# A windowed-attention and two-MLP kernel: another written order of the first part's tasks, and other engines for some of them

## Chip, cores and metric

One NeuronCore of a Trainium2 chip runs the kernel; the other cores are idle. The metric is the device time of one execution in microseconds (us), lower is better. Engines are named as in the profile: PE (TensorE matmul), PEld (its weight load), DVE (VectorE), ACT (ScalarE), POOL (GpSimd) and SP (SyncE, which here only issues DMA transfers). A name with q (SPq) is an engine's sequencer.

## What is computed

```python
# attention, B=4 H=8 S=576 D=64: a windowed one plus one on 4x down-sampled q, k, v
q_d, k_d, v_d = (t.reshape(B, H, S//4, 4, D).mean(axis=3) for t in (q, k, v))
out_up = np.repeat(softmax_attn(q_d, k_d, v_d), 4, axis=2)
mask = np.abs(pos[:, None] - pos[None, :]) < 4
out_local = softmax_attn(q, k, v, where=mask)
x = tokens_by_heads(out_up + out_local)      # (2304, 512)
h = x @ w_in                                 # 512 x 2048
y = (h * np.cos(h)) @ w_out                  # 2048 x 512
out = ((y @ w_a) * (y @ w_b)) @ w_out2       # 512 x 1536, 1536 x 512
```

All of it is in float32. The kernel makes a float32 product from three matmuls over a high and a low part of each operand.

## The kernel before, in words

**Two parts.** The first part holds the attention, the first MLP, and the preparation of the second MLP's weights. The second part, the second MLP, is a chain of matmuls whose operands are formed by ACT, POOL and DVE beside it; the change doesn't touch its instructions. In the first part everything is a *task* with a name, and a long string, `ORDER` (from line 48), lists 2663 task names. The loop at line 957 goes through the string and calls each task, and `InOrder.settle` (line 212) chains the instructions of each engine, SP among them, so that they run on the engine in just that written order. A suffix `@a`, `@d` or `@p` puts an operation on ACT, DVE or POOL where the kernel can do it on any of them.

**Attention tasks.** A unit u (0 to 7) is half a sequence of one batch entry; each has pairs of heads (last figure of a name). `lp` makes the local scores (PE, L402), `lm` masks them and takes the maximum (DVE, L409, L414), `lu` subtracts it (L419), `le`, `ln`, `lz` are the exponential, the sum and the division, `lt` transposes (PE, L497), `lc` copies the transposed scores out of PSUM (L299 on DVE, L297 on ACT). The same on down-sampled data is `sm` (sums of four, one instruction L379 on DVE or three, L381 to L383, on POOL), `dp` (PE, L426), `dx` (maximum, DVE, L432), `da`, `de`, `dn`, `dz`, `dt` (PE, L509), `dc`. `vp` sums v (PE, L350; `vs`, L370 on DVE, L372 and L374 on POOL, does this for later units). `at` multiplies by v (PE, L522, L529), `up` and `cb` (L545) combine both results in SBUF, `xh` and `xl` split them into high and low. One PSUM buffer named "att" holds scores, transposes or results of one step at a time.

**MLP tasks.** A group g (0 to 111) is 128 columns of the hidden layer for one block of tokens. `h{g}.0` to `.3` are its products (`h_mm`, three matmuls each, L595 to L597), in one of two PSUM buffers "h". Stages `c{g}.0` to `.5` make h·cos h: ACT L646, DVE L648, ACT L650, DVE L652 (which releases the PSUM buffer), then the high part (L297 or L299) and the low part (L658). `b{g}.0` to `.3` multiply by w_out into four accumulators, `e` and `S` copy out and store them.

**Weights.** They arrive as 64-bit words and are rebuilt: `w{n}.0` to `.4` for the first MLP (L273, L276 on ACT, L278 on DVE, then high and low). For the second MLP a block n (0 to 32) goes through `p{n}.0` (load, SP, L805), `.10`, `.11`, `.12` (rebuild, ACT L273 and L276, DVE L278), `.2` (four sums on POOL, L814 to L817) and `.5` (store, SP, L838). Below n = 24 the odd blocks share one buffer "praw" (a single one), and the even ones take whatever buffer of the pool "w" comes free, so a load waits on SP until an earlier block is stored.

Of the kernel before, what the change touches and what calls it, by code (L numbers as in the profile page):

```python
# [48 lines left out]
L0k0 L0k1 lp0.0 sm0.0@d L0w1 w1.1@a w1.0@a L0v0 sm0.1@d lm0.0 lu0.0@p dp0.0 dx0.0 L0k3 lu0.1@d da0.00@d da0.01@d le0.0 ln0.0 de0.0 dn0.0 dz0.1@a  # L49
dz0.0@d lz0.0@d L0V0 vp0.0 vq0.0@a vq0.1@a L0k2 sm0.2@d dt0.0 w1.2@d dc0.0@a L0w2 w2.0@a w2.1@a lt0.0 lc0.01@a lc0.00@d L0w0 w0.1@a L0w4 sm0.3@p  # L50
w1.3@d w1.4@p w2.2@d dp0.1 dx0.1 da0.10@d w0.0@a at0.0 up0.0@d cb0.1 cb0.0 w2.3@a w4.0@a w0.2@d w0.3@d da0.11@a w4.1@a w4.2@d w2.4@p L0v1 lp0.1 lm0.1
lu0.3@d lu0.2@d xh0.1@a w0.4@p L0w5 L0w6 w5.1@a w5.0@a w5.2@d xl0.1@d xh0.0@a xl0.0@p w6.0@a L0V1 vp0.1 w6.1@a Lc8 h0.0 Lc9 h0.1 de0.1 dn0.1 dz0.3@p
le0.1 ln0.1 vq0.3@a w6.2@d lz0.1@d Lk2.0 vq0.2@a Lq1.0 sm1.0@p Lq1.1 sm1.1@p dz0.2@a h1.0 h1.1 dt0.1 dc0.1@d w9.0@a w4.3@a lt0.1 lc0.10@d w9.1@a
w9.2@d w8.0@a w6.3@d w6.4@p lc0.11@a at0.1 up0.1@d cb0.2 L0w3 cb0.3 xh0.3@d w5.3@a w3.0@a w3.1@a xh0.2@a w8.1@a L0w7 w7.0@a xl0.2@d h0.2 Lc10 xl0.3@d
w7.1@a Lq1.3 Lk2.1 Lc11 Lw2.0 Lk2.2 Lc14 h0.3 w3.2@d w3.3@a w9.3@d w3.4@p w5.4@p w7.2@d c0.0@a c0.1@d lp1.0 lm1.0 lu1.1@d lu1.0@p w10.1@a h1.2 h1.3
dp1.0 c0.2@a c0.3@d w4.4@p c1.0@a c1.1@d w7.3@a c1.2@a dx1.0 Lq1.2 c0.4@a c1.3@d da1.00@d h2.0 da1.01@d h2.1 w7.4@d c0.5@p c1.4@d c1.5@p le1.0 w8.2@d
# [36 lines left out]
c33.0@a c33.1@d c33.2@a c33.3@d xh3.2@d c30.5@p lp4.0 lm4.0 lu4.0@d h32.2 h32.3 c32.0@a c32.1@d c32.2@a h34.0 h34.1 h34.2 Lp30 b28.0 b30.1 Lq4.2
c33.4@d lu4.1@p c33.5@d Lw4.3 b29.3 c32.3@d h34.3 c34.0@a c34.1@d vs4.3@p xl3.2@p dp4.0 dx4.0 da4.00@d da4.01@a b30.2 b29.0 Lw4.4 vs4.4@p b30.0 h35.0
# [1152 lines left out]
```

## Time and profile before

| | us |
|---|---|
| median of 3 runs (905.39 to 907.26) | 906.39 |
| the profiled execution | 908.52 |
| its span, first to last instruction | 906.8 |
| PE busy | 884.1 (97%) |
| DVE, ACT, POOL busy | 675.3, 559.3, 507.2 |
| mean granted clock of TensorE | 0.992 |

The span lies inside the execution's own time, with 1.7 us around it. PE is the busiest engine. A stall is written in a trace as the idle time in brackets ahead of an instruction, with the work that ended it. The first part ends near 515 us.

### The profile page before, as it was taken

The page shows a single profiled execution, that of the slowest core. Times are in us where ns is not written, and L with a number is a line of the kernel's source. Part 1 is how long each engine was busy: PE and PEld are TensorE (multiplying, and loading weights), DVE is VectorE, ACT ScalarE, POOL GpSimd, SP SyncE. Part 2 cuts the span into 40 slices and gives each one's busy share as a digit, 9 for nine tenths or more (in the row PEclk, how much of TensorE's full clock was granted, in tenths as well). Part 3 has the DMA queues.
Part 4 walks back from the last instruction along what each step waited for, and adds up shares of the span by engine and source line. Part 5 has one row for each costly group of instructions (what it writes and reads, how often), then busy time and mean ns, then how long its engine had stood idle before and what let it go on. Part 6 is the DMA issues. An engine that isn't in the chain of part 4 may idle for free.

```text
span 906.8 us, 19124 instructions
## 1 busy us (share of the span) xinstructions
PE 884.1 (97%) x7020; PEld 858.1 (95%) x7020; DVE 675.3 (74%) x1295; ACT 559.3 (62%) x1172; POOL 507.2 (56%) x662
## 2 busy tenths in 40 slices
PE   5899999999999999999999999999999999999998
PEld 5789899999998998999999999999999999999998
DVE  7999898775876877734766688778867787776764
ACT  6999876575586765634665355466654477545473
POOL 5687755653566556302464267654586663677540
PEclk9799999999999999999999999999999999999999
DMA  9793322543756656102978166676742456832631
GB/s 352 278 353 109 103 64 64 183 147 91 222 175 203 216 182 192 46 1 64 289 220 274 63 203 209 209 314 241 290 153 85 154 205 250 323 113 89 228 143 53
DMA packets 96909, 162.13 MB, mean 179 GB/s; under 512 B 6576, under 2 KB 62896, under 8 KB 96816
## 3 DMA queue, kind: packets, MB, share of 16 engines
q1 hardware_dynamic: 96816, 160.92, 52.0%
q8 instruction: 55, 0.90, 0.4%
q14 instruction: 38, 0.31, 0.1%
HBM read 127.66 MB, written 33.23 MB: 177 GB/s over the span
## 4 chain that ended last, share of the span: by engine, by line
PE 78%; DMA 8%; DVE 4%; ACT 4%; POOL 3%; issue 2%; SPq 0%; ACTq 0%; POOLq 0%; DVEq 0%
PE z L595 14%; PE z L597 14%; PE z L596 14%; PE h L595 5%; PE acc L595 5%; PE h L596 5%; PE h L597 5%; PE acc L597 5%; PE acc L596 5%; DMA praw<-in_w_b_dram 2%; DMA wd_a<-praw 2%; DMA vs<-in_vds_dram 1%; PE att L402 1%; DVE praw L278 1%; DMA praw<-in_w_out_dram 1%
## 5 line engine op out<-in xcount | busy, mean ns | idle before, releaser
L991 POOL TENSOR_TENSOR sb<-w,sb 128x256 fp32r<-128x256 f32 x154 | 124.7, 822 | 115.2 <-ACT sb L989 112.0
L595 PE MATMUL h<-xbig,w 128*128 128x288 f32 (+1 forms) x448 | 145.2, 324 | 5.3 <-DVE gs L652 3.5
L595 PE MATMUL acc<-gh,w 128*128 128x288 f32 (+1 forms) x448 | 144.2, 322 | 0.0
L596 PE MATMUL h<-xbig,w 128*128 128x288 f32 (+1 forms) x448 | 141.5, 316 | 0.0
L597 PE MATMUL h<-xbig,w 128*128 128x288 f32 (+1 forms) x448 | 141.0, 315 | 0.0
L596 PE MATMUL acc<-gl,w 128*128 128x288 f32 (+1 forms) x448 | 140.3, 313 | 0.3 <-POOL gl L658 0.2
L597 PE MATMUL acc<-gh,w 128*128 128x288 f32 (+1 forms) x448 | 140.1, 313 | 0.2 <-POOL w L588 0.2
L989 ACT ACTIVATE sb<-w 128x256 fp32r<-128x256 f32 x252 | 96.6, 415 | 50.1 <-PE z L597 39.8
L658 POOL TENSOR_TENSOR gl<-gs,gh 128x288 fp32r<-128x288 f32 (+1 forms) x62 | 59.1, 956 | 92.7 <-ACT gh L297 49.3
L596 PE MATMUL z<-xbig,sb 128*128 128x384 f32 x288 | 96.2, 334 | 0.0
L595 PE MATMUL z<-xbig,sb 128*128 128x384 f32 x288 | 96.2, 334 | 0.0
L597 PE MATMUL z<-xbig,sb 128*128 128x384 f32 x288 | 96.2, 334 | 0.0
L595 PEld LDWEIGHTS h<-xbig,w 128*128 128x128 f32 x448 | 84.8, 189 | 10.8 <-DVE gs L652 6.0
L595 PEld LDWEIGHTS acc<-gh,w 128*128 128x128 f32 x448 | 84.2, 188 | 3.8 <-issue 1.3
L650 ACT ACTIVATE gs<-gs,turn 128x288 f32<-128x288 f32 (+1 forms) x112 | 63.4, 568 | 38.3 <-DVE gs L648 37.5
L596 PEld LDWEIGHTS h<-xbig,w 128*128 128x128 f32 x448 | 85.1, 190 | 1.2 <-DVE xbig L569 0.2
L596 PEld LDWEIGHTS acc<-gl,w 128*128 128x128 f32 x448 | 84.3, 188 | 1.9 <-POOL gl L658 0.7
L597 PEld LDWEIGHTS h<-xbig,w 128*128 128x128 f32 x448 | 84.9, 190 | 1.0
L597 PEld LDWEIGHTS acc<-gh,w 128*128 128x128 f32 x448 | 84.2, 188 | 1.5 <-POOL w L588 0.4
L646 ACT ACTIVATE gs<-h,turn 128x288 int32<-128x288 f32 (+1 forms) x112 | 58.9, 528 | 41.9 <-PE h L597 38.8
L648 DVE SCALAR_TENSOR_TENSOR gs<-gs,h 128x288 f32<-128x288 int32 (+1 forms) x112 | 54.9, 492 | 38.7 <-ACT gs L646 38.3
L991 DVE TENSOR_TENSOR sb<-w,sb 128x256 fp32r<-128x256 f32 x98 | 62.1, 635 | 22.0 <-ACT sb L989 22.0
(177 smaller groups left out, 2381.5 us busy)
## 6 DMA issues: line engine op xcount, KB each, us to landing
w<-wd SPq DMA_DIRECT2D x63, 512.0 KB, 5.9
w<-wd_a SPq DMA_DIRECT2D x18, 512.0 KB, 6.9
w<-wd_b SPq DMA_DIRECT2D x18, 512.0 KB, 7.6
raw<-in_w_in_dram SPq DMA_DIRECT2D x16, 512.0 KB, 7.2
raw<-in_w_out_dram SPq DMA_DIRECT2D x16, 512.0 KB, 7.9
w<-wd_a SPq DMA_DIRECT2D x18, 384.0 KB, 7.7
w<-wd_b SPq DMA_DIRECT2D x18, 384.0 KB, 6.7
praw<-in_w_a_dram SPq DMA_DIRECT2D x12, 512.0 KB, 3.4
```

The costliest lines, as they stand in the source:

```text
L278: dve.scalar_tensor_tensor(out=lw if out is None else out, in0=hh, scalar=3, in1=lw, op0=ALU.logical_shift_left, op1=ALU.bitwise_or)
L402: pe.matmul(p[i][o, W * w:W * w + W], qt[u, 2 * pr + i][r, off:off + W], kt[u // 2, 2 * pr + i][r, BASE[half] + off:BASE[half] + off + W], ...
L595: i = pe.matmul(ps_out, lh, rh, start=start, stop=False, skip_group_check=more)
L596: pe.matmul(ps_out, lh, rl, start=False, stop=False, skip_group_check=more)
L597: pe.matmul(ps_out, ll, rh, start=False, stop=stop, skip_group_check=more)
L646: act.activation(out=gs[g].bitcast(I32), in_=hps[g], func=AF.Identity, scale=1.0 / (2.0 * math.pi), bias=turn[:, 0:1])
L648: dve.scalar_tensor_tensor(out=gs[g], in0=gs[g].bitcast(I32), scalar=-2.0 * math.pi, in1=hps[g], op0=ALU.mult, op1=ALU.add)
L650: act.activation(out=gs[g], in_=gs[g], func=AF.Sin, bias=turn[:, 1:2])
L658: eng.tensor_tensor(out=gl[g], in0=gs.pop(g), in1=gh[g].bitcast(F32), op=ALU.subtract)
L989: act.activation(out=t[:, 0], in_=blk, func=AF.Copy)
L991: (dve if nst[0] % (C["SD"] if G else C["SD0"]) == 0 else pool).tensor_tensor(out=t[:, 1], in0=blk, in1=t[:, 0].bitcast(F32), op=ALU.subtract)
```

## The change

Only the string `ORDER` differs: the same 2663 tasks in another order, with other engine marks. Two places of it, the start, and the lines around p9 to p11:

```diff
-L0k0 L0k1 lp0.0 sm0.0@d L0w1 w1.1@a w1.0@a L0v0 sm0.1@d lm0.0 lu0.0@p dp0.0 dx0.0 L0k3 lu0.1@d da0.00@d da0.01@d le0.0 ln0.0 de0.0 dn0.0 dz0.1@a
...
+L0k0 L0k1 lp0.0 sm0.1@d L0w1 w1.1@a w1.0@a lm0.0 L0v0 L0k3 sm0.0@p dp0.0 dx0.0 da0.01@a da0.00@d L0V0 vp0.0 lu0.1@p sm0.3@d lu0.0@p L0w2 le0.0 ln0.0
...
-Lw6.2 vs6.2@p lt5.1 lc5.11@a h61.2 h61.3 lc5.10@a c61.0@a b59.3 c61.1@d c61.2@a c61.3@d b59.0 dt5.1 dc5.1@a h63.0 h63.1 h63.2 c62.4@d h63.3 c63.0@a
-c61.4@a c61.5@d c62.5@p c63.1@d p11.0 p11.11 p11.10 p11.12 p11.2 h64.0 b59.1 h64.1 h64.2 b59.2 b60.2 c63.2@a c63.3@d h64.3 c64.0@a at5.1 up5.1@a b60.0
...
+xl5.1@d p10.0 p10.11 p10.10 p10.12 c62.4@a c62.5@d h63.0 p9.5 xl5.0@p h63.1 h63.2 c61.1@d h63.3 c63.0@a c63.1@d dt5.1 dc5.1@a b58.3 b59.3 b60.3 b58.1
+c61.2@a c61.3@d c61.4@d c61.5@d b59.0 p10.2 b59.1 c63.2@a at5.1 up5.1@a cb5.2 Lw6.2 vs6.2@p c63.3@d xh5.2@d xl5.2@d b59.2 cb5.3 p11.0 p11.10 p11.11
```

Operations by engine, before and after (a: ACT, d: DVE, p: POOL):

| task | before | after |
|---|---|---|
| `lu` | d 14, p 18 | d 5, p 27 |
| `sm` | d 18, p 14 | d 21, p 11 |
| `vs` | d 7, p 11 | d 4, p 14 |
| `e` (copies out) | a 24, d 16 | a 17, d 23 |
| `lc` | a 17, d 15 | a 20, d 12 |
| `xl` | d 10, p 22 | d 14, p 18 |
| `up` | a 6, d 10 | a 10, d 6 |

The number of matmuls is the same, and so is that of ACT's table loads (24).

**Start of POOL.** The first places on POOL after the constants (`smx` are local scores, `kd` and `qd` the sums of four, `w` a weight). Before:

```order
L675 MEMSET smd 72x12x16
L419 TENSOR_TENSOR smx<-smx,mx 128x5x64
L381 TENSOR_TENSOR kd<-kq 128x144
L382 TENSOR_TENSOR kd<-kd,kq 128x144
L383 TENSOR_TENSOR kd<-kd,kq 128x144
L381 TENSOR_TENSOR qd<-kq 128x72
L382 TENSOR_TENSOR qd<-qd,kq 128x72
L383 TENSOR_TENSOR qd<-qd,kq 128x72
L588 TENSOR_TENSOR w<-raw,w 128x512 x3
```

Now:

```order
L675 MEMSET smd 72x12x16
L381 TENSOR_TENSOR kd<-kq 128x144
L382 TENSOR_TENSOR kd<-kd,kq 128x144
L383 TENSOR_TENSOR kd<-kd,kq 128x144
L381 TENSOR_TENSOR qd<-kq 128x72
L382 TENSOR_TENSOR qd<-qd,kq 128x72
L383 TENSOR_TENSOR qd<-qd,kq 128x72
L419 TENSOR_TENSOR smx<-smx,mx 128x5x64 x2
L490 TENSOR_TENSOR smd<-smd,sd 72x6x48
L588 TENSOR_TENSOR w<-raw,w 128x512 x3
```

POOL's sums now belong to the first pair of heads (`sm0.0`, before `sm0.3`) and come first, and two subtractions `lu` follow instead of one.

**DVE behind the result of unit 1's first pair of heads** (`at1.0`; `xf<-att` are `up` and `cb`, `gs` the cosine, `sd` sums for a softmax, `w<-raw` a weight). Before:

```order
L299 COPY xf<-att 128x144
L648 SCALAR_TENSOR_TENSOR gs<-gs,h 128x288
L545 TENSOR_TENSOR xf<-att,xf 128x288
L480 TENSOR_SCALAR sd<-sd 72x4
L481 RECIPROCAL sd<-sd 72x4
L299 CAST w<-raw 128x512
L545 TENSOR_TENSOR xf<-att,xf 128x288
L652 TENSOR_TENSOR gs<-gs,h 128x288
```

Now:

```order
L648 SCALAR_TENSOR_TENSOR gs<-gs,h 128x288 x2
L299 COPY xf<-att 128x144
L545 TENSOR_TENSOR xf<-att,xf 128x288 x2
L480 TENSOR_SCALAR sd<-sd 72x4
L481 RECIPROCAL sd<-sd 72x4
L299 CAST w<-raw 128x512
L652 TENSOR_TENSOR gs<-gs,h 128x288
```

The two combining operations, behind which the PSUM buffer "att" is free, follow the copy at once, and the three others come after them.

**ACT from the rebuilding of p11 to that of p12** (the two `praw` rows at either end; `gs<-h` is the first stage of one MLP group). Before:

```order
L276 ACTIVATE praw<-praw,turn 128x512
L273 ACTIVATE praw<-praw 128x512
L650 ACTIVATE gs<-gs,turn 128x288
L646 ACTIVATE gs<-h,turn 128x288
L297 ACTIVATE xf<-att 128x144
L650 ACTIVATE gs<-gs,turn 128x288
L297 ACTIVATE xbig<-xf 128x288 x2
L273 ACTIVATE praw<-praw 128x512
L276 ACTIVATE praw<-praw,turn 128x512
```

Now:

```order
L273 ACTIVATE praw<-praw 128x512
L276 ACTIVATE praw<-praw,turn 128x512
L646 ACTIVATE gs<-h,turn 128x288
L650 ACTIVATE gs<-gs,turn 128x288
L297 ACTIVATE gh<-gs 128x288
L646 ACTIVATE gs<-h,turn 128x288
L650 ACTIVATE gs<-gs,turn 128x288
L297 ACTIVATE xbig<-xf 128x288
L646 ACTIVATE gs<-h,turn 128x288
L276 ACTIVATE praw<-praw,turn 128x512
L273 ACTIVATE praw<-praw 128x512
```

Three MLP groups begin between the two blocks where one did before.

## Rows read from the trace of the kernel before

**Rows 1.** The page: busy us of each engine, share of the span, instructions.

```profile
PE 884.1 (97%) x7020; PEld 858.1 (95%) x7020; DVE 675.3 (74%) x1295; ACT 559.3 (62%) x1172; POOL 507.2 (56%) x662
```

**Rows 2.** Stretches: from:to, length, busy us by engine, granted clock, DMA share, GB/s.

```profile
0.00:22.60 22.60, 13.23 (x230) 11.51 (x232) 16.46 (x40) 14.04 (x33) 11.88 (x25) 0.93 0.93 352
22.60:45.30 22.70, 20.37 (x259) 17.62 (x256) 20.88 (x46) 21.45 (x49) 15.79 (x20) 0.77 0.74 278
45.30:68.00 22.70, 21.43 (x312) 19.57 (x311) 21.97 (x47) 21.88 (x49) 19.21 (x23) 1.00 0.96 353
...
200.00:300.00 100.00, 97.34 (x1095) 93.54 (x1094) 69.52 (x148) 63.33 (x126) 53.62 (x93) 1.00 0.57 177
...
600.00:700.00 100.00, 100.00 (x576) 100.00 (x576) 77.78 (x135) 60.11 (x143) 63.38 (x69) 1.00 0.56 202
```

**Rows 3.** PE's timeline, stalls from 40 to 520 us: start, us, operation, [idle before].

```profile
43.30 0.40 PE L596 MATMUL acc<-gl,w 128*128 128x288 f32 x1 [0.17 <-POOL gl L658]
...
46.94 0.35 PE L426 MATMUL att<-kd,qd 64*72 64x144 f32 x2 [0.35 <-DVE qd L379]
...
57.15 0.41 PE L497 MATMUL att<-ident,smx 128*128 128x128 f32 x2 [0.91 <-DVE xf L545]
...
98.73 0.24 PE L509 MATMUL att<-ident,smd 72*112 72x72 f32 x1 [1.76 <-DVE smx L299]
...
275.70 0.28 PE L509 MATMUL att<-ident,smd 72*112 72x72 f32 x1 [0.40 <-ACT smx L297]
...
290.33 0.40 PE L595 MATMUL h<-xbig,w 128*128 128x288 f32 x1 [1.32 <-DVE gs L652]
```

**Rows 4.** What PE waited for up to 520 us: total us, times, longest.

```profile
PE h L595 <- DVE gs L652: 3.5, 5, 1.3
```

**Rows 5.** PE's timeline, two starts after a pause near the beginning.

```profile
20.44 0.37 PE L402 MATMUL att<-kq 64*64 64x64 f32 x2 [2.40 <-issue]
...
33.02 0.61 PE L595 MATMUL h<-xbig,w 128*128 128x288 f32 x1 [1.66 <-ACT xbig L297]
```

**Rows 6.** PE's timeline at the start: the first down-sampled scores (dp0.0).

```profile
6.64 1.24 PE L426 MATMUL att<-kd,qd 64*72 64x144 f32 x8
```

**Rows 7.** POOL's timeline at the start: last constant, six sums (first and last).

```profile
4.67 0.25 POOL L675 MEMSET smd<- 72x192 f32 x1
...
10.19 0.44 POOL L381 TENSOR_TENSOR kd<-kq 128x144 f32<-128x144 f32 x1
...
12.70 0.37 POOL L383 TENSOR_TENSOR qd<-qd,kq 128x72 f32<-128x72 f32 x1
```

**Rows 8.** DVE's timeline ahead of the stall at 98.73.

```profile
92.53 0.68 DVE L278 SCALAR_TENSOR_TENSOR raw<-raw 128x512 uint32<-128x512 uint32 x1
...
95.44 2.67 DVE L278 SCALAR_TENSOR_TENSOR raw<-raw 128x512 uint32<-128x512 uint32 x1
```

**Rows 9.** POOL's timeline beside the longer of the two.

```profile
96.01 1.55 POOL L658 TENSOR_TENSOR gl<-gs,gh 128x288 fp32r<-128x288 f32 x2
```

**Rows 10.** POOL's timeline: the first of four sums of p10, and of p17.

```profile
275.81 0.46 POOL L814 TENSOR_TENSOR praw<-praw 128x128 f32<-128x128 f32 x1 [2.18 <-DVE praw L278]
...
323.36 0.46 POOL L814 TENSOR_TENSOR praw<-praw 128x128 f32<-128x128 f32 x1 [0.82 <-DVE praw L278]
```

**Rows 11.** ACT's timeline: the rebuilding of p12, and of p19, begins.

```profile
286.45 0.67 ACT L273 ACTIVATE praw<-praw 128x512 f32<-128x512 f32 x1 [2.91 <-DMA praw<-in_w_a_dram]
...
331.76 0.80 ACT L276 ACTIVATE praw<-praw,turn 128x512 uint32<-128x512 uint8 x1 [0.39 <-DMA praw<-in_w_b_dram]
```

**Rows 12.** PE's timeline, one MLP product of three matmuls and the next one's start.

```profile
45.37 0.29 PE L596 MATMUL acc<-gl,w 128*128 128x288 f32 x1
...
45.77 0.29 PE L596 MATMUL acc<-gl,w 128*128 128x288 f32 x1
```

**Rows 13.** Line L419 (`lu`) by engine: ns min/median/max, first and last start.

```profile
L419 POOL TENSOR_TENSOR smx<-smx,mx x18: 717/738/1622, 8.6 to 356.7; 128x320 f32<-128x320 f32 x18
L419 DVE TENSOR_TENSOR smx<-smx,mx x14: 429/488/1018, 9.2 to 360.3; 128x320 f32<-128x320 f32 x14
```

More of the change, by code (lines that the diff above doesn't have):

```diff
@@ L53 @@
[L53 to L56, printed above, removed]
@@ L125 @@
-b61.0 c64.3@d lm6.0 c65.0@a c65.1@d c65.2@a p12.12 p12.2 dp6.0 dx6.0 p11.5 c65.3@d da6.01@d da6.00@a c65.4@a c65.5@p Lq7.1 h67.0 h67.1 h67.2 h67.3
-c67.0@a lu6.1@d c67.1@d h66.0 Lq6.2 sm6.2@d b62.0 b63.0 b62.2 b61.3 b61.1 b62.1 sm6.3@p p13.0 p13.10 e63.0@a h66.1 h66.2 p13.11 p13.12 c67.2@a c67.3@d
-c64.4@a Lw6.3 h66.3 b62.3 c66.0@a c66.1@d c66.2@a p12.5 vs6.3@d p14.0 c64.5@p h68.0 h68.1 lu6.0@p p13.2 b63.2 e63.2@d h68.2 c66.3@d h68.3 c68.0@a
-c68.1@d b63.1 e63.1@a lp6.1 lm6.1 c66.4@a c66.5@d p14.10 p14.11 p14.12 p14.2 S63.0 b63.3 Lw6.4 h69.0 e63.3@a h69.1 c68.2@a c68.3@d c67.4@a c67.5@p
@@ L137 @@
-p18.2 b73.3 cb6.1 xh6.1@d b74.3 c76.4@a xh6.0@d b72.0 p19.0 p19.11 p19.10 c75.4@d c75.5@d lt6.1 lc6.11@a lc6.10@d b73.0 xl6.0@p p19.12 p19.2 h78.0
-h78.1 h78.2 p18.5 h78.3 c78.0@a h77.3 c77.0@a c77.1@d XH1@a dt6.1 b73.2 c76.5@d dc6.1@a xl6.1@p c78.1@d b73.1 b74.1 b75.1 b76.1 c77.2@a c77.3@d
-c77.4@d c77.5@d p20.0 p20.10 p20.11 at6.1 up6.1@d cb6.3 xh6.3@a xl6.3@p h79.0 XL1@d h79.1 h79.2 h79.3 b75.3 p19.5 p21.0 p20.12 p20.2 p20.5 b74.0 b75.0
-cb6.2 b77.1 c78.2@a c78.3@d c79.0@a c79.1@d b74.2 XH2@a XL2@d xh6.2@d xl6.2@p lp7.0 lm7.0 Lq7.3 b75.2 b76.2 c78.4@a c78.5@p c79.2@a c79.3@d c79.4@d
@@ new lines @@
+xl5.1@d p10.0 p10.11 p10.10 p10.12 c62.4@a c62.5@d h63.0 p9.5 xl5.0@p h63.1 h63.2 c61.1@d h63.3 c63.0@a c63.1@d dt5.1 dc5.1@a b58.3 b59.3 b60.3 b58.1
+c61.2@a c61.3@d c61.4@d c61.5@d b59.0 p10.2 b59.1 c63.2@a at5.1 up5.1@a cb5.2 Lw6.2 vs6.2@p c63.3@d xh5.2@d xl5.2@d b59.2 cb5.3 p11.0 p11.10 p11.11
+h65.0 h65.1 p10.5 h65.2 h65.3 b60.1 h64.0 h64.1 h64.2 p11.12 p11.2 c65.0@a c65.1@d lp6.0 h64.3 c65.2@a c65.3@d c65.4@a c65.5@p b60.2 h67.0 lm6.0
+c64.0@a c64.1@d c64.2@a c64.3@d b60.0 b61.0 h67.1 h67.2 h67.3 Lw6.3 vs6.3@p dp6.0 c63.4@d c63.5@p xh5.3@a c67.0@a c67.1@d p12.0 p12.11 dx6.0 p11.5
@@ new lines @@
+p12.10 p12.12 h66.0 h66.1 h66.2 h66.3 sm6.3@d Lq6.2 b61.1 b62.1 c66.0@a da6.00@a Lq7.0 b61.2 b62.2 lu6.0@p b63.1 c66.1@d Lw6.4 p12.2 p13.0 c67.2@a
+c66.2@a b63.2 b61.3 b62.3 e63.1@a xl5.3@p b62.0 Lv6 e63.2@a c67.3@d p12.5 lu6.1@d c66.3@d c66.4@d c64.4@d c64.5@p da6.01@a b63.3 e63.3@a c66.5@d S63.3
+S63.1 h68.0 h68.1 p13.11 p13.10 p13.12 p13.2 b63.0 p14.0 vs6.4@p c67.4@a h68.2 h68.3 c68.0@a h69.0 c68.1@d p13.5 sm6.2@d b64.3 h69.1 h69.2 h69.3
+c68.2@a c68.3@d Lw6.5 e63.0@a S63.2 b64.1 c69.0@a c69.1@d lp6.1 lm6.1 b64.0 h70.0 le6.0 ln6.0 b64.2 b65.2 c67.5@p h70.1 h70.2 Lq7.1 h70.3 lu6.2@p
@@ new lines @@
+b65.1 c68.4@a c68.5@d Lq7.2 b65.3 b66.3 p14.11 p14.10 p14.12 p14.2 lz6.0@p c70.0@a c70.1@d c69.2@a b65.0 b66.0 lu6.3@p c69.3@d b66.1 dp6.1 b66.2 b67.2
+b68.2 c70.2@a c70.3@d c70.4@a p15.0 h72.0 h72.1 dx6.1 da6.10@d sm7.1@d c69.4@a c69.5@p h71.0 da6.11@a S63.0 h72.2 p14.5 c70.5@d p16.0 p15.10 p15.11
+p15.12 p15.2 h72.3 c72.0@a c72.1@d h71.1 h71.2 h71.3 c71.0@a c71.1@d vs6.5@p c72.2@a lt6.0 lc6.00@d lc6.01@d b67.3 b68.3 b67.1 b67.0 b68.0 b69.0
+c71.2@a b68.1 de6 c72.3@d sm7.0@p c71.3@d c71.4@d h73.0 c71.5@p p15.5 b70.0 h73.1 c72.4@d c72.5@d h74.0 dn6 dz6.1@p p17.0 p16.11 p16.10 p16.12 p16.2
@@ new lines @@
+c78.1@d xl6.0@p b75.3 dt6.1 dc6.1@d b73.2 h77.0 h77.1 c76.4@a h77.2 h77.3 c78.2@a c77.0@a c76.5@p at6.1 c78.3@d c78.4@d c78.5@d c77.1@d c77.2@a p17.5
+up6.1@d cb6.3 xh6.3@d xl6.3@p h79.0 XL1@p h79.1 h79.2 h79.3 b74.1 cb6.2 b74.2 p19.0 p19.10 p18.5 c77.3@d p20.0 p19.11 XH2@d p19.12 p19.2 b75.2 b76.2
+b74.0 c79.0@a c79.1@d b75.0 lp7.0 xh6.2@a xl6.2@d b76.0 XH3@a XL3@d c79.2@a c79.3@d lm7.0 lu7.1@p c77.4@a c77.5@d b75.1 b76.1 p20.10 b76.3 h80.0
+c79.4@a Lv7 p20.11 p20.12 Lq7.3 h80.1 h80.2 h80.3 c80.0@a c80.1@d c80.2@a b77.2 b78.2 lu7.0@p h81.0 h81.1 h81.2 h81.3 c79.5@d b79.2 p19.5 p21.0
@@ new lines @@
+c80.3@d XL2@p c81.0@a c81.1@d c81.2@a p20.2 p20.5 dp7.0 dx7.0 da7.00@d da7.01@a p21.10 sm7.2@d e79.2@d S79.2 b77.1 b78.1 b79.1 h82.0 h82.1 h82.2 h82.3
+e79.1@d S79.1 c81.3@d c80.4@a c80.5@d b77.0 p21.11 p21.12 sm7.3@p p21.2 c82.0@a c82.1@d c82.2@a le7.0 lp7.1 lm7.1 lu7.2@p h84.0 h84.1 b77.3 b78.3
+b79.3 lu7.3@p e79.3@a b78.0 b79.0 e79.0@a c82.3@d ln7.0 p22.0 dp7.1 c81.4@a c81.5@p h84.2 h84.3 h83.0 p22.10 dx7.1 da7.11@d lz7.0@p da7.10@d h83.1
+c84.0@a c84.1@d b80.2 p21.5 b81.2 le7.1 ln7.1 c82.4@d c82.5@p p22.11 p22.12 de7 p22.2 b80.1 b81.1 dn7 dz7.0@p lt7.0 lc7.00@d c84.2@a c84.3@d h83.2
@@ new lines @@
+h95.1 h95.2 h95.3 b89.3 xl7.2@p c90.4@a c90.5@p b89.1 b89.2 c94.0@a c94.1@d b89.0 c94.2@a c94.3@d c94.4@d c94.5@d c95.0@a c95.1@d c95.2@a c95.3@d
+h96.0 h96.1 h96.2 h96.3 h97.0 h97.1 h97.2 h97.3 b90.2 p25.0 c91.4@d c91.5@p b90.3 b90.1 c96.0@a b90.0 b91.0 b91.3 c96.1@d c96.2@a c96.3@d h98.0 h98.1
+h98.2 h98.3 p24.3 b91.1 b91.2 p24.4 p24.5 c92.4@d c92.5@d b92.3 p25.10 p25.11 p25.12 c97.0@a c97.1@d c97.2@a b92.2 b92.0 b93.0 b94.0 p25.2 c97.3@d
+c95.4@d c95.5@d p27.0 p28.0 b93.2 p25.3 p25.4 c98.0@a b92.1 b93.1 p25.5 p27.11 c98.1@d c98.2@a b93.3 c97.4@d c97.5@d c98.3@d p27.10 p27.12 p28.10
```

208 lines of the change are left out of this document (99 added, 109 removed).

## The prediction

> **What bounds the kernel now.** I read the stretches of the span first [rows 2]. The reader is to see three regimes in them. Up to 68 us PE is busy 55.0 of 68.0 us, and from 22.6 us DVE and ACT are busy 42.9 and 43.3 of 45.4 us: there all three engines stand at their limit, and the small operations of the attention decide. From 200 to 300 us PE has 97.3 of 100 us while DVE has 69.5 and POOL 53.6: PE is the limit, with a few stalls. From 600 us, in the second part, PE has 100.0 of 100. Over the span PE is busy 97% [rows 1], so nearly everything that a new order can give lies in the pauses and in the clock.
>
> Second, PE's own timeline, filtered to starts with idle time ahead [rows 3]. From 40 us to the end of the first part there are eleven stalls. Five lie between 43 and 99 us: 0.17, 0.35, 0.91 and 1.76 us, and another of the same length as the first, 3.36 us in all. Six lie between 254 and 446 us. The table of waits gives five of them in one line, 3.5 us for products that wait for a PSUM buffer "h", which DVE's L652 releases [rows 4]; the sixth is 0.40 us [rows 3]; so 3.90 us. Together 7.26 us: the most that removing stalls behind 40 us can give.
>
> Third, the granted clock. The first two stretches have means of 0.93 and 0.77 [rows 2]. At two levels, 1.2 and 2.4 GHz, a mean of 0.93 over 22.6 us is 3.2 us at the lower one, and 0.77 over 22.7 us is 10.4 us: 13.6 us, which fall into two pieces of 6.8 us. One begins while PE waits 2.40 us and the other while it waits 1.66 us [rows 5].
>
> **The change part by part.** Both kernels issue the same matmuls, so PE's own work costs nothing more or less. The sum is made against the profiled execution, 908.52 us, which is 2.13 us above the median of the runs, 906.39.
>
> *The start, to 40 us.* Two things pull apart. The sums of four of the first pair of heads go from DVE to POOL. There they are six instructions, 10.19 to 13.07 us, so 2.88 us [rows 7]; behind the last constant, which ends at 4.92, they end no earlier than 7.80, while the first down-sampled scores, which need them, start at 6.64 now [rows 6]. So those scores are 1.2 us late, and behind them, on PE, the sums over v; but the local scores come ahead of them in both orders. On the other side the order of the combining steps of the first pair lets the second pair's local scores, now behind the pause of 2.40 us [rows 5], start somewhat sooner; at best that pause goes and gives 2.4. The bounds are therefore 1.2 lost and 2.4 won. I take 0.4 won, near nothing, because from 22.6 us on DVE and ACT are busy 95% of the time [rows 2] and the work that they have to do ahead of the second block's products hardly changes: what PE gains at 20 us it would wait for at 33. **-0.4 us.**
>
> *From 40 to 100 us.* Three stalls lose their cause. The transposes at 57.15 wait 0.91 us [rows 3] for the second combining step, which stands behind two small operations and a cast on DVE; now both combining steps follow each other directly, so the buffer "att" is free earlier by those three. The transposes at 98.73 wait 1.76 us for a copy on DVE, which stands behind a rebuilding of a weight that took 2.67 us instead of the 0.68 of another one of the same shape [rows 3, 8]; now one of the two copies is on ACT, and no such rebuilding stands ahead of them. The 0.35 at 46.94 also goes, since the sums that it waits for are written earlier. That is 3.02 us of the 3.36. But the new order has tight places of its own: the local scores of unit 1 come one product behind the last result of unit 0, which two combining steps must first take out of the same buffer; the result of unit 1's first pair stands close behind its transposes; and a product follows closely on the transposes of unit 2. I charge these three at the mean of the five stalls of now, 0.67 us each, 2.0 in all. **-1.0 us.** The ends are -3.4 (no new ones) and +2.3 (three of 1.76 against the 3.02).
>
> *From 200 to 450 us.* Blocks of weights for the second part pass through few buffers. From the first sum of block p17 on POOL to the rebuilding of p19 in the same buffer, with the store and the load between, it takes 323.36 to 331.76, so 8.4 us; for p10 to p12 it took 275.81 to 286.45, so 10.6 us [rows 10, 11]. ACT, which runs in written order, stands idle if less work than that lies between: before p12 it did so for 2.91 us, and 4 us later PE stalled 1.32 us at 290.33 [rows 3, 11]. How much time the written order leaves is counted in PE's groups of three matmuls, 0.40 us each [rows 12], longer ones in proportion, with the steps of the attention between. Of the 24 distances between blocks that follow each other in a buffer, p0 to p25, before six are under 8.4 us: p10 6.3, p11 5.2, p17 7.9, p19 6.3, p20 6.4, p22 7.4; they lack 10.9 us in all. Now two are under it: p6 8.2 and p8 6.1, lacking 2.5 us. At 10.6 us a chain, before lacks 28.5 us and now 11.1. So the ACT pauses shrink to between a quarter and two fifths. The row of ACT between p11 and p12 shows it: three groups begin there where one did. A second cause of these stalls, sums over v that are written right behind the load of their data, goes too: the shortest distance from such sums to the next ones grows from 0.8 to 3.1 us of PE work. I take it that all but two of the six stalls go, at their mean of 0.65 us: 3.9 less 1.3. **-2.6 us**, between -3.9 and 0 (if other stalls come in their place).
>
> *Operations on other engines.* Nine `lu` in the balance go to POOL: at the median 9 x 0.488 = 4.4 us less for DVE and 9 x 0.738 = 6.6 us more for POOL [rows 13]. Three sums over v go the same way, four `xl` the other way, seven copies out (`e`) from ACT to DVE, and a few more. Behind 100 us these cost nothing, since work of PE covers them: DVE has 30 us in 100 to spare and POOL 46 [rows 2]. If that cover is gone, each is worth its own duration, under 1 us. Ahead of 68 us they are already in the terms above, apart from what the rival below says. *The second part:* nothing changes there and PE is at 100 in 100 [rows 2]: 0.
>
> The sum is -0.4 - 1.0 - 2.6 = -4.0, so 904.5 for an execution like the profiled one, and 906.39 - 4.0 = **902.4 us** for the median.
>
> **A rule weighed against the trace.** The row first: a rebuilding on DVE took 2.67 us where another took 0.68, and POOL was at work beside it on an operation with two inputs in SBUF [rows 8, 9]; and `lu` on POOL took up to 1.62 us where its median is 0.74 [rows 13]. So one meeting costs the two engines up to 2.0 and 0.9 us here. The Trainium skill, page "SBUF — State Buffer", section "Who interferes with whom", says that DVE and GpSimd share one pair of ports, that a DVE instruction with two SBUF inputs contends with a GpSimd one that reads SBUF, and that whoever is second blocks for the whole instruction. It speaks against moving `lu` to POOL, whose operands are both in SBUF. By the rule each of the nine could block DVE for its own 0.74 us, and the sum would be up to 6.6 us worse in DVE's time; by the rows most of that falls where DVE has time to spare. The long rows agree with the rule in kind, not in size.
>
> **The rivals.** *The stalls only move.* The new order is as tight as the old one elsewhere, and stalls of the same size come where now none are. For it: DVE and ACT have as much to do as before ahead of 68 us, and two block distances still fall short. Against it: the distances above are longer nearly everywhere. Then only the start's 0.4 and a tenth of the stalls are won: 905.7 us, no change that can be measured.
>
> *DVE loses time in the first 68 us.* The place is that stretch, where DVE is busy 42.9 of 45.4 us, so a microsecond lost there is one of PE. Three more `lu` of units 0 and 1 run on POOL there. If each meets a DVE operation as at 95.44 and stretches it by 2.0 us [rows 8], 6.0 us are lost: 902.4 + 6.0 = 908.4 us, slower. It decides from the third meeting on; two give 906.4, no change. For it: the 1.62 in [rows 13] is from just this stretch, at 8.6 us. Against it: most `lu` on POOL are at 0.72 to 0.74, and at the start DVE's work beside them now is maxima and copies from PSUM.
>
> *A stretch of low clock goes too.* If one of the two pauses of [rows 5] becomes short enough that the clock stays up, 6.8 us at half speed become at best 3.4: 902.4 - 3.4 = 899.0 us. For it: the start is what was reordered most. Against it: PE waits there for engines that are 95% busy and do the same work.
>
> *The order does nothing* (transfers, not the order, set the stalls) gives 906.4; it is counted with the first rival.
>
> **How the numbers follow.** The forecast has 0.50, moved stalls 0.22, lost DVE time 0.16, the clock 0.12. A change can be told from none by about 0.2%, 1.8 us. The forecast and the clock are faster by more: 0.62. Moved stalls are within: 0.22. Lost DVE time is slower: 0.16. The forecast's own range is 900.4 to 904.4: half of what it wins more or less. The range for 8 in 10 reaches down to the clock's 899.0 and up to 907.6, past the moved stalls and short of the three meetings.
>
> **What would show it.** Right: no stall over 0.7 us on PE between 57 and 100 us from a combining step or a copy of DVE; ACT's idle time ahead of `praw` operations shrunk to under half, and the line "h waits for gs, L652" near 1 us instead of 3.5; the second part as long as before. The first down-sampled scores start near 7.9 us, and unit 1's local scores show a new stall of up to 1 us. The granted clock of the first two stretches stays near 0.93 and 0.77. Wrong: a mean clock that differs there by over 0.1 (then the clock decides, either way); L278 or L419 rows of over 1.5 us before 68 us, with PE waiting behind them; new stalls of more than 3 us in all from 100 to 500 us.

## The result

| | before | after |
|---|---|---|
| median, us (6 runs each) | 906.46 (905.39 to 907.87) | 898.86 (897.15 to 899.96) |
| profiled execution, us | 908.52 | 898.67 |
| its span, us | 906.8 | 896.8 |

The ratio is 0.9913 (95% interval 0.9898 to 0.9928): faster by 7.6 us between the medians, 7.9 by the ratio. The direction was forecast, the size was not: 4.0 us were predicted. 898.86 lies 1.5 us below the forecast's own range (900.4 to 904.4) and 0.14 us below the range for 8 in 10 (899.0 to 907.6). The two profiled executions are 9.85 us apart, because the one before was 2.1 us above its median and the one after 0.2 below. Where the profiles are compared below the sum is therefore 9.9 us, not 7.6.

The profile after, stretches (from:to, length, busy us of PE, PEld, DVE, ACT, POOL, granted clock, DMA share, GB/s), to be held against [rows 2]:

```profile
0.00:22.60 22.60, 13.68 (x257) 11.51 (x259) 16.23 (x39) 15.27 (x41) 12.91 (x28) 1.00 0.92 348
22.60:45.30 22.70, 17.04 (x248) 14.97 (x244) 20.44 (x48) 21.50 (x44) 13.55 (x13) 0.92 0.71 262
45.30:68.00 22.70, 21.11 (x307) 18.98 (x303) 20.48 (x46) 21.63 (x48) 19.02 (x22) 1.00 1.01 392
200.00:300.00 100.00, 100.00 (x1122) 96.75 (x1121) 72.68 (x157) 68.44 (x131) 55.21 (x101) 1.00 0.62 188
600.00:700.00 100.00, 100.00 (x578) 100.00 (x577) 77.12 (x137) 57.21 (x139) 66.00 (x74) 1.00 0.52 184
```

From 200 to 300 us PE is now busy in all of the time, where it had 97.34 us before. PE's timeline after, every start with over 0.1 us of idle time ahead between 40 us and the end of the first part, against [rows 3]:

```profile
40.30 0.81 PE L402 MATMUL att<-kq,q 64*64 64x64 f32 x40 [0.30 <-PE h L597]
...
46.52 0.40 PE L595 MATMUL h<-xbig,w 128*128 128x288 f32 x1 [0.36 <-DVE gs L652]
...
51.58 0.56 PE L509 MATMUL att<-ident,smd 72*112 72x72 f32 x6 [0.65 <-DVE smx L299]
...
52.81 0.60 PE L522 MATMUL att<-smd,vd 48*64 48x72 f32 x24 [0.24 <-ACT smd L297]
...
56.79 0.40 PE L595 MATMUL h<-xbig,w 128*128 128x288 f32 x1 [0.35 <-DVE gs L652]
```

Eleven stalls of 7.26 us have become five of 1.90 us, and behind 57 us there is none. The second part is unchanged. Its first matmul, before and after:

```profile
508.79 0.33 PE L595 MATMUL z<-xbig,sb 128*128 128x384 f32 x1
```

```profile
499.11 0.34 PE L595 MATMUL z<-xbig,sb 128*128 128x384 f32 x1
```

So 9.7 of the 10.0 us between the spans are won ahead of it. Where they are won shows when both traces are read at equal PE work: the written order gives the work ahead of every MLP product, and the trace its start.

| start of the same work, before, us | after, us | lead, us |
|---|---|---|
| 48.4 | 46.7 | 1.7 |
| 55.7 | 55.2 | 0.5 |
| 93.8 | 92.4 | 1.4 |
| 106.0 | 102.8 | 3.3 |
| 228.3 | 225.0 | 3.3 |
| 260.6 | 256.0 | 4.6 |
| 293.8 | 286.9 | 6.9 |
| 335.9 | 327.6 | 8.4 |
| 447.5 | 437.5 | 10.0 |
| 506.3 | 496.6 | 9.7 |

1.7 us come from the start, 1.6 between 48 and 106 us, and 6.4 between 228 and the end of the part, in steps at the places where the kernel before stalled. This is one execution of each kernel. How far two executions can mislead shows in start_new below: its profiled one is 4.1 us under that of the kernel before (904.45 against 908.52), while their medians differ by 0.3 us.

### The profile page after: what moved, and what is told of

Same layout as the page of the kernel before. It is cut to its first block, busy times and chain, and to the rows that moved or that the text cites. A ratio compares the mean times of both kernels' runs of the same rounds, so it can differ in the third digit from the quotient of the medians.

```text
span 896.8 us, 19112 instructions
## 1 busy us (share of the span) xinstructions
PE 877.1 (98%) x7020; PEld 853.9 (95%) x7020; DVE 666.3 (74%) x1290; ACT 561.3 (63%) x1175; POOL 504.4 (56%) x669
## 4 chain that ended last, share of the span: by engine, by line
PE 94%; ACT 2%; DVE 2%; POOL 1%; issue 1%; POOLq 0%; ACTq 0%
PE z L597 15%; PE z L596 15%; PE z L595 15%; PE acc L595 8%; PE h L595 8%; PE acc L597 7%; PE acc L596 7%; PE h L596 7%; PE h L597 7%; PE att L426 1%; PE att L402 1%; PE att L529 1%; PE att L497 1%; PE att L522 1%; PE att L509 1%
## 5 line engine op out<-in xcount | busy, mean ns | idle before, releaser
L991 POOL TENSOR_TENSOR sb<-w,sb 128x256 fp32r<-128x256 f32 x154 | 124.9, 825 | 115.5 <-ACT sb L989 106.0
L658 POOL TENSOR_TENSOR gl<-gs,gh 128x288 fp32r<-128x288 f32 (+1 forms) x60 | 55.0, 922 | 72.7 <-DVE gh L299 47.2
L652 DVE TENSOR_TENSOR gs<-gs,h 128x288 f32<-128x288 f32 (+1 forms) x112 | 54.9, 492 | 35.8 <-ACT gs L650 35.3
```

Of the source, the lines that this page charges most:

```text
L652: dve.tensor_tensor(out=gs[g], in0=gs[g], in1=hps[g], op=ALU.mult)
L658: eng.tensor_tensor(out=gl[g], in0=gs.pop(g), in1=gh[g].bitcast(F32), op=ALU.subtract)
L991: (dve if nst[0] % (C["SD"] if G else C["SD0"]) == 0 else pool).tensor_tensor(out=t[:, 1], in0=blk, in1=t[:, 0].bitcast(F32), op=ALU.subtract)
```

## The experiments

Twelve kernels were run in three rounds, each beside new runs of the kernel before on the same chip (medians 906.70, 906.11 and 906.68 us). The ratio is to those runs, with its 95% interval, and a gain in us is the ratio's. A hybrid takes a number of tasks from the head of one order and all others in the other order; its seam is the place between. Code cuts show of long lines only the part that changes, and "..." stands for what is left out.

| run | what it is | median, us | ratio |
|---|---|---|---|
| start_new | new start, then old | 906.42 | 0.9993 (0.9980 to 1.0007) |
| mid_new | new from 46 to 176 us | 907.07 | 0.9997 (0.9986 to 1.0008) |
| late_new | old to 176 us, then new | 905.12 | 0.9982 (0.9971 to 0.9993) |
| late2 | old to 229 us, then new | 911.65 | 1.0056 (1.0041 to 1.0071) |
| early2 | new to 229 us, then old | 904.79 | 0.9986 (0.9973 to 1.0000) |
| pvs_old | new, weight blocks at old places | 935.35 | 1.0314 (1.0291 to 1.0336) |
| engines_new | old order, new marks | 942.38 | 1.0391 (1.0368 to 1.0415) |
| order_new | new order, old marks | 944.47 | 1.0410 (1.0395 to 1.0426) |
| no_hold | old, short buffer chain | 902.84 | 0.9959 (0.9943 to 0.9975) |
| edits | old, two tasks moved | 905.55 | 0.9984 (0.9974 to 0.9994) |
| edits_no_hold | both | 901.67 | 0.9939 (0.9925 to 0.9953) |
| after_no_hold | new, short buffer chain | 899.51 | 0.9920 (0.9906 to 0.9934) |

**Hybrids by stretch.** Theory: the lead of the table above can be cut out by stretch. Rivals: it is the clock of the start, or a stall is worth its idle time alone. The seam of the first:

```diff
-h3.3 c3.0@a b0.0 b1.0 lu1.3@p sm1.3@d c2.3@d c3.1@d
...
+w10.2@d dz1.1@p w8.3@a c2.2@a Lk2.2 lu1.2@p c3.0@a b0.0
```

> The kernel before with the new order (and engine marks) of its first 204 tasks alone, up to the first products of unit 0's third and fourth groups (about 46 us); all later tasks in the old order. Theory (the gain is removed stalls behind 40 us, each of which costs more than its idle time in brackets; in the profile the start leads by 1.7 us only): 1.5 to 2 us faster, about 904.7 us, clock of the first two 22.6 us stretches near 1.00 and 0.92. Rival (the clock at the start is most of the gain: 10 us less at half speed): 4 to 5 us faster, about 902 us.

> The kernel before with the new order from about 46 to about 176 us alone. Theory: only the stalls at 57 and 99 us go, with 0.7 us of new ones coming: 1 to 1.6 us faster, about 905.2 us, and the six stalls from 250 to 450 us stay. Rival (the lead of the profile comes from the old start's place, so that without the new start the middle gives nothing): 906.4 us.

> The kernel before with the new order from about 176 us on alone. Theory: all six stalls from 250 to 450 us go, and each gives more than its idle time, from the lead of the profile 6.4 us instead of 3.9: 4.5 to 6.4 us faster, about 901 us; clock at the start as in the kernel before. Rival (a stall is worth its idle time): 3.9 us faster at most, 902.6 us.

All three fell short of the theory. The gains, 0.6, 0.3 and 1.6 us, of which the first two can't be told from none, don't add up to 7.9. The seams spoil them at least in part: late_new stalls for 2.56 us at 184.8 us, just behind it, in its profile, mid_new has stalls of 0.2 to 0.8 us behind its two seams. But late_new has no other stall behind 100 us, so the new order of the late part does take all six away. The cut at 229 us, where the two orders have done nearly the same tasks, was to be cleaner:

```diff
-h51.3 c51.0@a h53.0 dc4.1@d at4.1 c51.1@d
...
+h51.3 c51.0@a h53.0 dc4.1@d Lq5.3 S47.0 p4.0 c51.1@d at4.1
```

> The kernel before to its 1330th task (about 229 us, where both orders have done all but five of the same tasks), then the new order. Theory (late stalls, each worth more than its idle time): no stall behind 229 us, 5 to 6.5 us faster than the kernel before, about 901 us; the stalls at 57 and 99 us and the low clock of the start stay. Rival (the earlier late_new, 1.6 us faster, was not spoiled by the 2.8 us stall at its seam, but shows the worth of the late part): 905 us.

> The counterpart: the new order to its 1331st task, then the old one. Theory: start and middle as in the changed kernel, 2 to 3 us faster than the kernel before, about 904 us, with four to six stalls left between 250 and 450 us; together with late2 the gains add up to the 7.6 us of the change. Rival (the late stalls depend on the start's times, so a new start takes them away): 901 us or less.

It was worse. late2's timeline of PE has this as its only stall behind 100 us:

```profile
245.86 0.61 PE L595 MATMUL h<-xbig,w 128*128 128x288 f32 x1 [8.19 <-DVE gs L652]
```

Without it late2 would be at 911.65 - 8.2 = 903.5 us, 2.6 us under the kernel before, an estimate. early2 keeps two of the six late stalls (0.51 us at 252.5, 0.57 at 287.1), where four to six were expected, and has one of 1.47 us at 243.7 that neither parent has; less that, its gain of 1.3 us is 2.8, an estimate too. The hybrids show that none of the six is left where the late part is new; for their worth they are too rough.

**Weight blocks back at their old places.** The tasks p0 to p21, and the loads and sums over v of units 4 to 6, moved in the new order:

```diff
-xl5.1@d p10.0 p10.11 p10.10 p10.12 c62.4@a c62.5@d h63.0 p9.5 xl5.0@p
...
+b57.0 p9.5 p10.11 p10.10 p10.12 vs6.1@d p10.2 b58.0 xh5.0@a b57.2
```

> The changed kernel, in which only the tasks of the second part's weights p0 to p21 and the loads and sums over v of units 4 to 6 are put back to the places that they had before, counted in PE's work; everything else stays in the new order. Theory (the distance between blocks in a buffer sets the late stalls): p10, p11, p17, p19, p20 are short again by 2 to 3 us, ACT waits again for praw, and three or four stalls of 0.4 to 1.3 us come back: 2 to 4 us slower than the changed kernel, 901 to 903 us. Rival (the stalls went because of the other order of products and cosine stages, which leaves more slack per PSUM buffer h): under 1 us slower, 899 to 900 us.

Against the changed kernel it lost 36 us instead of 2 to 4, with stalls of up to 5.4 us. The blocks matter, but at the old places they also stand among other operations of ACT, DVE and POOL than they did before. So it doesn't tell the two theories apart.

**Marks and order apart.** The first line of the string in engines_new:

```diff
-L0k0 L0k1 lp0.0 sm0.0@d L0w1 w1.1@a w1.0@a L0v0 sm0.1@d lm0.0 lu0.0@p dp0.0 dx0.0 L0k3 lu0.1@d da0.00@d da0.01@d le0.0 ln0.0 de0.0 dn0.0 dz0.1@a
+L0k0 L0k1 lp0.0 sm0.0@p L0w1 w1.1@a w1.0@a L0v0 sm0.1@d lm0.0 lu0.0@p dp0.0 dx0.0 L0k3 lu0.1@p da0.00@d da0.01@a le0.0 ln0.0 de0.0 dn0.0 dz0.1@p
```

order_new is the reverse: each task of the new order with the mark that it had before.

> The kernel before in its old order, with only the engine marks of the changed kernel. Theory (the order wins, the marks are worth little, since PE's work covers them behind 100 us): 905.5 to 908 us. Rival one (the marks take load from DVE where it sets the stalls): 903 us or less. Rival two (POOL's added subtractions block DVE's operations): 909 us or more.

> The changed kernel's order with the engine marks of the kernel before. Theory (an order fits only its own marks, as the old order with the new marks lost 36 us): over 10 us slower than the kernel before, with stalls all over the first part. Rival (the order alone carries the gain): 899 to 903 us.

Either half alone loses 36 to 38 us. In engines_new the table of PE's waits begins like this (us in total, times, longest), with PE held by the same release as in [rows 4] but 19 times:

```profile
PE h L595 <- DVE gs L652: 13.6, 19, 2.3
...
PE h L596 <- POOL xbig L569: 4.1, 1, 4.1
PE att L426 <- POOL qd L383: 3.5, 2, 2.5
```

Both expectations that priced the order or the marks alone missed. The number of engines_new lies with its rival two, but that rival's cause isn't shown: the longest `lu` on POOL in it takes 1.17 us, and the table names mostly DVE's L652. Order and marks can't be priced apart. My pricing of the marks at nothing, "since work of PE covers them", fits the new order, behind whose 57 us PE has no stall; for a mark by itself it isn't shown, and in the old order the marks as a whole are not covered.

**The buffer chain alone.** The cleanest test leaves the order as it is and shortens the chain of sums, store and load. The store of a block p0 to p23 sends a constant tile in the same pieces, so the block's buffer is free behind its sums; the second part then computes with other numbers.

```diff
-                parts_ = ((flat.bitcast(F32)[:, :896], wd[nm, p][:, :, js]),)
+                parts_ = ((None, wd[nm, p][:, :, js]),)
             for src, dst in parts_:
-                sp.dma_start(out=dst, in_=src.rearrange("p (b c) -> p b c", c=128))
+                sp.dma_start(out=dst, in_=ident[:, None, :].to_broadcast([128, 7, 128]) if src is None else src.rearrange("p (b c) -> p b c", c=128))
```

> The kernel before in the old order, but the stores of the prepared weights p0 to p23 send a constant tile in the same pieces instead of the block, so that a block's buffer is free after its sums and not after its store; the second part then multiplies by other numbers. Theory (the buffer chain of sums, store and load of 8.4 to 10.6 us sets the late stalls): the chain is about 5.5 us, shorter than all distances but p11's, so ACT's waits for praw shrink to under 5 us in all and the stalls at 254, 276, 290, 355 us go; 3 to 5.5 us faster than the kernel before, about 902.5 us. Rival (the transfers themselves are late, or other work of ACT and DVE makes the stalls): under 1 us faster.

It is faster by a ratio of 0.9959, 3.7 us. ACT's waits for these blocks up to 520 us (total, times, longest), first in the kernel before, 23.3 us in all:

```profile
ACT praw L273 <- DMA praw<-in_w_b_dram: 6.6, 4, 3.0
...
ACT praw L273 <- DMA praw<-in_w_a_dram: 4.5, 2, 2.9
ACT praw L276 <- DMA praw<-in_w_b_dram: 4.4, 5, 1.5
...
ACT praw L273 <- DMA praw<-in_w_out_dram: 3.4, 2, 1.9
ACT praw L276 <- DMA praw<-in_w_out_dram: 3.2, 2, 2.9
...
ACT praw L276 <- DMA praw<-in_w_a_dram: 1.2, 2, 0.8
```

In no_hold, 10.2 us, of which 5.9 are blocks behind p23 (w_out), whose stores were left as they are:

```profile
ACT praw L276 <- DMA praw<-in_w_out_dram: 3.3, 2, 2.7
...
ACT praw L273 <- DMA praw<-in_w_out_dram: 2.6, 2, 1.5
...
ACT praw L276 <- DMA praw<-in_w_b_dram: 1.9, 1, 1.9
...
ACT praw L273 <- DMA praw<-in_w_a_dram: 0.9, 1, 0.9
...
ACT praw L273 <- DMA praw<-in_w_b_dram: 0.8, 1, 0.8
ACT praw L276 <- DMA praw<-in_w_a_dram: 0.7, 1, 0.7
```

And in the changed kernel, 3.0 us:

```profile
ACT praw L276 <- DMA praw<-in_w_b_dram: 1.3, 2, 0.7
...
ACT praw L273 <- DMA praw<-in_w_out_dram: 0.9, 1, 0.9
...
ACT praw L273 <- DMA praw<-in_w_a_dram: 0.5, 1, 0.5
...
ACT praw L276 <- DMA praw<-in_w_out_dram: 0.3, 1, 0.3
```

The reader is to see that the new order shrinks these waits, as the experiment does by a shorter chain. Of the six late stalls two are left in no_hold's trace, of 0.76 us at 274.65 and 0.23 us at 440.65; the other four went, among them the one at 315.62, which the expectation doesn't name. The first of the two is that at 275.70 before, which it does. Ahead of it ACT still waits 1.86 us for a block, and SP, idle since 257.3, issued that block's load only behind a load of v (`vs`):

```profile
267.21 0.33 SPq L333 DMA_DIRECT2D vs<-in_vds_dram  x1
267.65 0.36 SPq L805 DMA_DIRECT2D praw<-in_w_b_dram  x1
```

SP's own waits between 255 and 275 us show what held the load of v, sums over v on POOL (L374):

```profile
SPq L333 <- POOL vd L374: 12.0, 2, 9.8
```

So in this trace it is the second cause that the prediction names, sums over v, that holds the load through SP's written order, and a shorter chain doesn't help. It doesn't always stall PE: in edits_no_hold SP waits as long, but ACT only 0.73 us and PE not at all. What this cause costs was not measured by itself.

**Two tasks of DVE alone.**

```diff
-cb1.0 xh1.0@a b2.2 dn1.1 dz1.2@p Lc23 w11.3@d cb1.1
+cb1.0 cb1.1 xh1.0@a b2.2 dn1.1 dz1.2@p Lc23 w11.3@d
...
-lt2.1 lc2.11@d w16.2@d dz2.3@p c12.5@p w22.0@a w23.0@a c13.4@a c13.5@p lc2.10@d
+lt2.1 lc2.11@d lc2.10@d w16.2@d dz2.3@p c12.5@p w22.0@a w23.0@a c13.4@a c13.5@p
```

> The kernel before with two tasks moved on DVE and nothing else: the second combining step of unit 1's first pair (cb1.1) directly behind the first one, and the second copy of unit 2's transposes (lc2.10) directly behind the first, ahead of the rebuilding w16.2. Theory: the stalls at 57 us (1.07 us over the pace of products) and at 99 us (1.9 us) go, 2.5 to 3 us faster, about 903.5 us. Rival (the time is lost again a little later, as DVE has the same work): under 1 us faster.

> The same two moves, and stores of the prepared weights p0 to p23 from a constant tile as in no_hold. Theory (causes are independent and add): 3.3 us of no_hold and those of the two moves, 5.5 to 6.3 us faster than the kernel before, about 900.3 us, so most of the change's 7.6 us without its order. Rival (they overlap): 902 us or more.

The two moves give 0.9984, 1.5 us, about half of what was expected. The stall at 57 us falls from 0.91 to 0.19 us and that at 99 us goes, but the next product pays a part, as PE's timeline of edits shows:

```profile
57.03 0.40 PE L595 MATMUL h<-xbig,w 128*128 128x288 f32 x1 [0.39 <-DVE gs L652]
```

```profile
99.98 0.40 PE L595 MATMUL h<-xbig,w 128*128 128x288 f32 x1 [0.27 <-DVE gs L652]
```

Together with the short chain the ratio is 0.9939, 5.5 us: 1.5 and 3.7 make 5.2, so within the intervals the two causes add. No stall over 0.1 us is left in that trace behind 101 us.

**The chain in the new order.**

> The changed kernel with stores of p0 to p23 from a constant tile. Theory (in the new order the buffer chain binds nowhere any more): within 1 us of the changed kernel, 898 to 900 us. Rival (part of the chain is still paid without showing as a stall): 897 us or less.

0.9920 against 0.9913: the same within the intervals. In the new order the chain costs nothing any more that can be measured. None of the twelve beats the changed kernel.

## Why the prediction was wrong in size

*The direction and the mechanisms.* The late stalls come from the chain of sums, store and load against the distance in the written order; no_hold shortens the chain and gives 3.7 us in the old order, and nothing measurable in the new one. The stalls at 57 and 99 us come from what stands between two steps on DVE; the two moves take away the second and most of the first. Together that is 5.5 of the 7.9 us. For the other 2.4 no experiment shows a cause.

*Which terms failed.* The late term (2.6 us) and the sum of start and middle (1.4 us) both came out too small. The medians can be divided by early2 at 229 us: about 2.8 us for start and middle, and so about 5 us for the late part, an estimate, to which no_hold alone gives 3.7.

*The late term, -2.6, was mis-sized.* "I take it that all but two of the six stalls go, at their mean of 0.65 us": no stall is left behind 57 us, and the lead grows by 6.4 us behind 228 us in the profiles. Two things were missed. The two distances still under 8.4 us (p6, p8) stall PE nowhere: ACT's waits for blocks shrank from 23.3 to 3.0 us, an eighth, where a quarter to two fifths were forecast, and PE's waits for L652 have 0.71 us left behind 40 us, all of it ahead of 57. And idle time in brackets is less than a stall costs: at 290.33 the bracket says 1.32 us [rows 3], but from the matmul before to this one it is 1.62 us where products follow at 0.13 us [rows 12], so 1.49 are lost. Worked out in the same way the six lose 4.9 us against 3.9 in brackets; the rest of the 6.4 is spread over shorter delays. In the medians it is less. The profiled execution of before was 2.1 us above the median, and I took its stalls as those of every run. Other kept traces with the old order in this stretch stall less between 250 and 450 us: 3.5 us in edits, 2.1 in start_new and in mid_new and 1.1 in early2, against 3.9 (their order ahead of it differs).

*The middle, -1.0.* The profiles show -1.6, the two moves 1.5 in the medians. Of the three new places that I charged with 0.67 us each, the local scores of unit 1 (0.73 us at 32.0) lie ahead of this stretch, and the result behind the first transposes of unit 1 pays 0.24 us at 52.81; the product behind unit 2's transposes pays nothing. So 2.0 us were charged for what cost 0.24 in this stretch, though stalls that weren't forecast came at 40.30, 46.52, 51.58 and 56.79, 1.66 us in all. For the stall at 98.73 the text has one of the two copies on ACT and no rebuilding ahead of them; that reading is wrong. The rebuilding w16.2 stood between lc2.11 and lc2.10; it now stands ahead of both, and both copies are still on DVE.

*The start, -0.4.* The profiles show -1.7 at 48 us. The down-sampled scores are late as forecast, and there are pauses:

```profile
7.86 1.24 PE L426 MATMUL att<-kd,qd 64*72 64x144 f32 x8 [0.62 <-POOL qd L383]
...
18.76 1.10 PE L402 MATMUL att<-kq 64*64 64x64 f32 x38 [1.50 <-issue]
...
25.74 0.57 PE L596 MATMUL h<-xbig,w 128*128 128x288 f32 x1 [2.10 <-POOL xbig L569]
...
32.03 0.81 PE L402 MATMUL att<-kq,q 64*64 64x64 f32 x40 [0.73 <-issue]
...
36.27 0.71 PE L426 MATMUL att<-kd,qd 64*72 64x144 f32 x8 [1.38 <-DVE smx L409]
...
38.14 0.40 PE L595 MATMUL h<-xbig,w 128*128 128x288 f32 x1 [1.15 <-DVE gs L652]
```

The first and the fourth are the 7.9 us and the new stall of up to 1 us that the text named. The pause ahead of 18.76 is 0.9 us shorter than that in [rows 5], and though PE waits at other places instead (25.74, 36.27, 38.14), not all of that gain is given back. What the start gives in the medians isn't settled: start_new can't be told from no change, with a stall of 0.40 us behind its seam and 0.45 us left of the one at 57 us; 7.9 us by the ratio, less the 5.5 of edits_no_hold, leaves 2.4 us for the start and all else.

*The clock rival, 899.0.* The number came close, and the text's own sign for it came true: the mean clock of the second stretch differs by 0.15 (0.92 against 0.77), where over 0.1 was to mean that the clock decides. Yet the other runs speak against it. The profiles' low stretches shrank from 13.6 us to 22.7 x 0.08 x 2 = 3.6 us. But runs of the same kernel differ as much: after_no_hold, with the same start, has these two stretches:

```profile
0.00:22.60 22.60, 13.88 (x265) 11.81 (x266) 16.26 (x39) 15.30 (x41) 12.97 (x28) 1.00 0.94 351
22.60:45.30 22.70, 17.26 (x221) 15.12 (x218) 19.03 (x46) 20.23 (x42) 12.14 (x12) 0.77 0.64 232
```

That is 10.4 us at the lower level again, 6.8 more than in the changed kernel, and its execution took 900.04 us, only 1.4 us more than the profiled one of the changed kernel. The other way round, edits has the order of the kernel before up to 55 us, and its trace has 6.8 us less at the lower level:

```profile
0.00:22.60 22.60, 12.98 (x225) 11.43 (x227) 16.05 (x39) 13.71 (x32) 11.46 (x25) 0.95 0.93 353
22.60:45.30 22.70, 18.79 (x267) 16.22 (x264) 21.71 (x48) 22.53 (x51) 16.77 (x21) 0.90 0.76 288
```

Yet it starts the scores that stand at 46.94 in [rows 3] only 0.53 us sooner:

```profile
46.41 0.47 PE L426 MATMUL att<-kd,qd 64*72 64x144 f32 x4 [0.33 <-DVE qd L379]
```

So 6.8 us less at the lower level went with 0.5 to 1.4 us, and not with the rival's 3.4. Over the runs the mean clock is 0.9943 before (61 runs) and 0.9967 after (6 runs), so 10.3 and 5.9 us at the lower level. For these 4.4 us the clock's part is then 0.3 to 0.9 of the 7.6 us, an estimate. The 61 times of the kernel before say much the same, though weakly: a line through them falls by 0.23 us (standard error 0.11) for each 0.001 of mean clock, 0.6 us for the 0.0024. The forecast was wrong in leaving the clock of the start as it was, but most of the 7.6 us isn't the clock.

*DVE's time in the first 68 us.* The rival did not come. In the changed kernel POOL's `lu` took at most 1.18 us, and no rebuilding of a weight over 1.24:

```profile
L419 POOL TENSOR_TENSOR smx<-smx,mx x27: 722/730/1181, 9.1 to 350.5; 128x320 f32<-128x320 f32 x27
```

```profile
L278 DVE SCALAR_TENSOR_TENSOR raw<-raw x32: 658/684/1241, 15.2 to 150.5; 128x512 uint32<-128x512 uint32 x32
```

## What to carry to other kernels

Where engines run in a written order and data pass through one or two buffers, count the time of a buffer's whole round (work, store, load) in the trace, and the bottleneck engine's work between two rounds in the order; a place where the second is shorter may stall. Six were shorter before, and four of the six stalls went when the chain was shortened; two are shorter now, and PE stalls at neither. Price a stall by the distance between starts, or by the lead at equal work, rather than by the idle time in brackets, and take several executions' times before its size is taken as given. An order and its choice of engines are one thing: either alone cost more here (36 to 38 us) than the whole change won.

## What the runs showed of the hardware that I had not expected

The time at the lower clock varies from run to run of the same kernel: in six runs of the changed one the mean clock was 0.994 to 1.000, that is 0 to 10.8 us at the lower level, with 899.9 us at 0.994, 897.37 at 0.996 and 897.15 us at 1.000. In the traces shown it lies in the first 45 us, and the same start had means of 0.93 and 0.77 there in one execution (before) and 0.95 and 0.90 in another (edits).

The rebuilding of 2.67 us on DVE [rows 8] is no chance event. In all seven traces with the old order and marks from 60 to 100 us (edits among them) the longest rebuilding of such a weight takes 2.22 to 2.68 us, and in the four with the new ones (after, after_no_hold, early2, mid_new) at most 1.52. It was 2.24 us in edits:

```profile
94.93 2.24 DVE L278 SCALAR_TENSOR_TENSOR raw<-raw 128x512 uint32<-128x512 uint32 x1
```

beside this row of POOL, the last of a run without a gap since 92.86:

```profile
95.04 1.58 POOL L658 TENSOR_TENSOR gl<-gs,gh 128x288 fp32r<-128x288 f32 x2
```

In both kernels DVE's instruction ends 0.55 us after POOL's run does: 98.11 against 97.56 before [rows 8, 9], 97.17 against 96.62 here. 0.68 us is what it takes by itself, so it looks as if it did nearly nothing until POOL was through. The Trainium skill, page "SBUF — State Buffer", section "Who interferes with whom", says that a DVE instruction with two SBUF inputs contends with a GpSimd one that reads SBUF, and calls the port pair that they share an exclusive lock. These rows fit that, with a wait that outlasts more than one of POOL's instructions. That POOL's run is the cause was not tried by itself.
